# Scores one phase further ahead, PSUM copies on VectorE and a new product order in a fused attention and feed-forward kernel on Trainium2

## The chip, the cores and the metric

The kernel runs on one core of a Trainium2 chip. The core has five engines with queues of their own: TensorE (matrix products, "PE" in the profile, its weight loads "PEld"), VectorE ("DVE"), ScalarE ("ACT"), GpSimd ("POOL") and SyncE ("SP"). Each works through its instructions in program order and waits on semaphores for the others. Products land in PSUM, everything else lives in SBUF, and DMA engines move data to and from DRAM. The metric is the device time in microseconds (us) from the first to the last instruction of a run, with what lies around it. Lower is better.

## The reference

```python
def _attn_ref(q, k, v):            # 8 batches, 8 heads, 576 positions, 64 wide
    ...
    scores = scale * np.matmul(q_c, k_c.transpose(0, 1, 2, 4, 3))
    ...
    attn = np.exp(scores)
    attn = attn / (np.sum(attn, axis=-1, keepdims=True) + 1e-09)
    out = np.matmul(attn, v_c)

def _moe_ref(x, w_in, w_out, beta):
    h = x @ w_in                                # 4608x512 by 512x2048
    g = h * (1.0 / (1.0 + np.exp(-beta * h)))
    return (g @ w_out).astype(np.float32)       # by 2048x512
```

Attention runs inside chunks of 64 positions. Its 8 x 576 rows, 512 wide, go through a feed-forward layer with the activation `g`.

## The kernel before

The 4608 rows are cut into nine blocks of 512 tokens, `j` = 0 to 8; a block holds eight chunks. Every block goes through the same stages.

**Attention.** `emit_T` (L126) turns a quarter of one batch's queries and keys on VectorE. `emit_sc` (L142) makes the scores of half a block on TensorE (64 small products) into two PSUM tiles `sc0`, `sc1`, and ScalarE takes their exponentials into `et`. `emit_pv` (L174) multiplies a quarter of a block (128 tokens) by the values on TensorE, in the one PSUM tile `x`; VectorE then takes a reciprocal (L201) and scales (L203), which frees the tile; a DMA from SyncE transposes the result into `xt` (L211), the block's input to the first layer. The loads come from GpSimd's queue: `load_v` (L93), four DMAs a batch, and `load_qk` (L83), two.

**First layer, `L1` (L533).** Of the 16 hidden units (128 features each) eight are made directly: `emit_m` makes four products of 512 columns (`emit_h`, L244) and an activation on ScalarE (L254). The other eight are made by two calls of `unit` (L282), each a seven-product scheme for 2x2 blocks: bank A takes four products one upon the other, and after each of the first three a copy of the running sum is taken (`u1`, `u2`, `u3`, helper `snap`); B and C (in the tile `x`) take one and two products. The scheme needs four differences of the input, `xs` (`emit_xs`, L271, on VectorE), combines `t = u3 + w1` on GpSimd (L329) and `c1` on VectorE (L331, L335), and ends in six activations (L311). `u1` is copied by ScalarE (L306), the other copies by VectorE (L308). Direct units (`spacers`) stand between the products. A unit's bank A lies in `sc0` or `sc1`.

**Second layer, `steps_L2` (L381).** It is the seven-product scheme once more, on `g`'s halves: `mm0` to `mm6`, each of 16 products of 256 columns (L398), bank A again with running copies on ScalarE (`take`, L409), results combined on VectorE (`cB`, `cD`, `cC`, L417) and on GpSimd (`w1`, L443, and the last sum, L463). It needs sixteen sums `s1` to `s4` of `g` (`emit_sum`, four parts each): `s3` on GpSimd (L362), the others on VectorE (L358, L360, L364).

**The order** is written out by hand at L636 to L688: between the products of block `j`'s second layer stand the scores and the PV of block `j`+1. Half the scores come ahead of `mm0`, the other half after `mm1`, the four PVs after `mm1`, `mm2`, `mm3` and `mm4`; the turns of the batch after next (`tr`) stand between them, and the loads at the end. Block 0 runs a plain form of both layers, ahead of which the weights are loaded.

Of the kernel before, what the change touches and what calls it, by code (L numbers as in the profile page):

```python
# [11 lines left out]
ALU = mybir.AluOpType  # L12
# [3 lines left out]
def kernel(  # L16
# [265 lines left out]
    def unit(j, q, spacers):  # L282
        x = xt_t[j]
        ts = xs_t[j]
        up_, dn_ = slice(0, HT), slice(HT, BLK)
        b11, b21, b22 = x[:, 0:2, up_], x[:, 2:4, up_], x[:, 2:4, dn_]
        swr = [t.rearrange("p k (m i r) -> p k m r i", r=2, i=128) for t in sw]
        a11, a12, a22 = w_r[0][:, 0::2], w_r[0][:, 1::2], w_r[1][:, 1::2]
        bank = {"A": ps_s.tile([128, 2, HT], FP32, tag=f"sc{q}", name="wA")}
        xx = ps_x.tile([128, 2, 2, HT], FP32, tag="x", name="wX")  # L290
        bank["B"], bank["C"] = xx[:, 0], xx[:, 1]
        sb = {}

        def prod(b, a, rhs, first):
            for i in range(2):
                for kk in range(2):
                    nc.tensor.matmul(  # L297
                        out=bank[b][:, i, :], lhsT=a[:, kk, q, i, :], rhs=rhs[:, kk, :],
                        start=(first and i == 0 and kk == 0), stop=(kk == 1),
                        skip_group_check=True,  # L300
                    )

        def snap(nm, b, eng):
            sb[nm] = u_p.tile([128, 2, HT], FP32, tag=nm, name=nm)
            if eng == "a":
                nc.scalar.copy(out=sb[nm], in_=bank[b])  # L306
            else:
                nc.vector.tensor_copy(out=sb[nm], in_=bank[b])  # L308

        def silu(m, cols, src):  # L310
            nc.scalar.activation(  # L311
                out=gt_t[j][:, m, cols], in_=src, func=ACTF.Silu,
                scale=beta2[:, m % 2, m // 2:m // 2 + 1],
            )
# [7 lines left out]
        snap("u2", "A", "v")  # L322
        prod("C", swr[0], ts[0], True)
        snap("w1", "C", "v")
        spacers[1]()
        prod("A", swr[2], ts[2], False)
        snap("u3", "A", "v")
        sb["t"] = u_p.tile([128, 2, HT], FP32, tag="t", name="t")
        nc.gpsimd.tensor_tensor(out=sb["t"], in0=sb["u3"], in1=sb["w1"], op=ALU.add)  # L329
        prod("B", a12, b21, True)  # L330
        nc.vector.tensor_tensor(out=c1[:, :, up_], in0=bank["B"], in1=sb["u1"], op=ALU.add)  # L331
# [18 lines left out]
    def emit_sum(j, which, part):  # L350
# [2 lines left out]
        s1, s2, s3, s4 = s_t[j]  # L353
        g = gt_t[j]
        lo, hi = slice(2 * part, 2 * part + 2), slice(NM + 2 * part, NM + 2 * part + 2)
        tt = (nc.gpsimd if which == 3 else nc.vector).tensor_tensor
        if which == 1:
            tt(out=s1[:, lo], in0=g[:, lo, dn], in1=g[:, hi, dn], op=ALU.add)  # L358
        elif which == 2:
# [14 lines left out]
    def store(j, half, cols, t):  # L374
# [3 lines left out]
            in_=t,  # L378
        )

    def steps_L2(j, last=False):  # L381
        g = gt_t[j]
        t1, t2, t3, t4 = tw
# [9 lines left out]
        def prod(name, a, b, first, rows=(0, 1)):  # L393
            if first and name not in bank:
                grab(name)
            for i in rows:
                for kk in range(NM):
                    nc.tensor.matmul(  # L398
                        out=bank[name][:, i, :],
                        lhsT=a[:, kk, i * 128:(i + 1) * 128],  # L400
                        rhs=b[:, kk, :],
                        start=(first and i == 0 and kk == 0),
                        stop=(kk == NM - 1),
                        skip_group_check=True,
                    )

# [21 lines left out]
            prod("B", g[:, NM:KFF, up], b21, True)  # L428

        def mm2():  # L430
            prod("A", s_(2), t2, False)
            take("u2", "A")

        def mm3():
            prod("D", g[:, NM:KFF, dn], t4, True)

        def mm4():
            prod("A", s_(3), t3, False)
            take("u3", "A")
            if last:  # L440
                return
            sb["w1"] = u_p.tile([128, 2, HM], FP32, tag="w1", name="w1")
            nc.gpsimd.tensor_tensor(out=sb["w1"], in0=sb["u2"], in1=sb["u3"], op=ALU.subtract)  # L443

        def mm5():
            if not last:
                prod("C", s_(4), b22, True)
                return
            prod("E", s_(1), t1, True)
            for r, other in ((1, "u3"), (0, "u2")):  # L450
                if r:
                    store(j, 1, 1, comb("E", sb[other]))
                else:
# [79 lines left out]
    def L1(j, hooks={}, first=None):  # L533
# [7 lines left out]

        if first:
            first()
        emit_xs(j)
        unit(j, 0, [sp(8), sp(9), sp(10)])
        sp(11)()
        for p in (0, 2):
            emit_sum(j, 3, p)
        unit(j, 1, [sp(12), sp(13), sp(14)])
        for p in (1, 3):  # L550
# [4 lines left out]
        dve(4)  # L555
        hooks.get(KFF, lambda: None)()

    with tc.manual_schedule():
# [77 lines left out]
        for j in range(1, NB):  # L636
            na = j + 1
            hooks = {}
            if na < NB:
                hooks[KFF] = lambda: emit_sc(2 * na)  # L640
            if j == 1:
                T2 = T_items(2)
                hooks.update({9: T2[0], 11: T2[1], 13: T2[2], 15: T2[3]})
            L1(j, hooks, (lambda: emit_xp(7)) if j == 1 else None)
            at = []
            if na < NB:
                at = [
                    lambda: emit_pv(4 * na), lambda: emit_sc(2 * na + 1),
                    lambda: emit_pv(4 * na + 1), lambda: emit_pv(4 * na + 2),
                    lambda: emit_pv(4 * na + 3),  # L650
                ]
            tr = T_items(j + 2) if j + 2 < B else []
# [6 lines left out]
            mm[0]()  # L659
            while fill:  # L660
                dve()
            mm[1]()
            cB()
            go(at)
            go(at)
            emit_sum(j, 4, 0)
            emit_sum(j, 4, 1)
            mm[2]()
            go(tr)
            go(at)  # L670
            emit_sum(j, 4, 2)
            emit_sum(j, 4, 3)
            mm[3]()
            go(at)
            go(tr)
            mm[4]()
            cD()
            go(at)
            go(tr)
            mm[5]()  # L680
            if j < NB - 1:
                cC()
            go(tr)
            mm[6]()
            if j + 2 < B:
                load_v(j + 2)
            if j + 3 < B:
                load_qk(j + 3)  # L688


# [28 lines left out]
```

## Time and profile before

| what | before |
|---|---|
| median of 8 runs | 331.97 us (331.49 to 335.39) |
| the profiled execution | 331.78 us |
| its span in the trace | 330.0 us |
| around the span | 1.78 us |
| busy: TensorE, VectorE, ScalarE, GpSimd | 275.7, 222.7, 171.0, 140.0 us |
| mean granted TensorE clock | 0.984 |

The rows below are read like this. A timeline row has the start and the duration in us, the engine, the line, the operation, what it writes and reads, how many instructions are merged in it, and in brackets how long the engine sat idle before it and on whom it waited. A matmul's modelled end overlaps the next one's start, so the distance between two starts is what a product takes. A row of a table by windows has, for each stretch of the span, its length, the busy time and number of instructions of each engine, the granted clock, the DMA share and GB/s.

### The profile page before, as it was taken

How to read it: one execution, taken by the hardware profiler on the slowest of the kernel's cores; microseconds unless marked ns; L12 is line 12 of the kernel's file. 1: busy time of each engine (PE TensorE's matmuls, PEld its weight loads, DVE VectorE, ACT ScalarE, POOL GpSimd, SP SyncE). 2: the span in 40 equal slices, each digit the busy share in tenths (PEclk: the TensorE clock that was granted, in tenths of full speed). 3: DMA queues.
4: the chain of work that ended last, by engine and by line, in shares of the span. 5: the costliest groups of instructions: out<-in, count | busy, mean ns of one | idle time of the engine just before them, and what ended most of it. 6: DMA issues, size and time to landing. Idle time of an engine off the chain costs nothing.

```text
span 330.0 us, 8211 instructions
## 1 busy us (share of the span) xinstructions
PE 275.7 (84%) x3520; PEld 189.9 (58%) x3520; DVE 222.7 (67%) x377; ACT 171.0 (52%) x288; POOL 140.0 (42%) x130
## 2 busy tenths in 40 slices
PE   2889976688986998699878988899879987998695
PEld 0464433345864686468645865477547754875475
DVE  3653668859992799379836994499748565856573
ACT  1278046067347744664276526471667166716630
POOL 8622499344066415641464246431743124322430
PEclk9999999699999999999999999799999999999999
DMA  7999999400359234922493249314901310151012
GB/s 121 181 208 212 184 203 221 105 1 2 66 134 168 45 66 126 175 45 64 122 166 61 50 113 171 75 42 93 135 0 48 85 64 0 44 90 64 1 34 95
DMA packets 69589, 31.99 MB, mean 97 GB/s; under 512 B 53681, under 2 KB 63921, under 8 KB 69553
## 3 DMA queue, kind: packets, MB, share of 16 engines
q0 software_dynamic: 44960, 18.35, 45.3%
q1 hardware_dynamic: 24448, 12.99, 15.0%
q8 instruction: 27, 0.44, 0.6%
q10 hardware_dynamic: 144, 0.13, 0.1%
q14 instruction: 10, 0.07, 0.1%
HBM read 36.71 MB, written 9.44 MB: 140 GB/s over the span
## 4 chain that ended last, share of the span: by engine, by line
PE 39%; ACT 15%; POOL 14%; DMA 14%; DVE 10%; issue 6%; POOLq 0%; DVEq 0%
PE oA L398 14%; ACT gt L311 11%; DMA w_out<-in_moe_w_out_dram 10%; POOL t L329 6%; PE oD L398 4%; PE oB L398 4%; PE hps L244 4%; POOL vb L98 4%; PE wA L297 4%; DVE u L308 2%; DMA ku<-in_k_dram 2%; DMA xt<-x 2%; PE x L186 2%; PE wX L297 2%; DVE xs L277 2%
## 5 line engine op out<-in xcount | busy, mean ns | idle before, releaser
L244 PE MATMUL hps<-xt,wi 128*128 128x512 f16 (+1 forms) x336 | 82.6, 376 | 5.0 <-DMA xt<-x 3.9
L254 ACT ACTIVATE gt<-hps,beta 128x512 f16<-128x512 f32 x80 | 54.3, 688 | 44.2 <-PE hps L244 44.1
L362 POOL TENSOR_TENSOR s<-gt 128x512 f16<-128x512 f16 x32 | 39.5, 1255 | 48.0 <-ACT gt L311 48.0
L244 PEld LDWEIGHTS <-wi 128*128 128x128 f16 x336 | 32.7, 100 | 31.0 <-DMA xt<-x 5.8
L308 DVE COPY u<-wA 128x512 f32<-128x512 f32 x32 | 22.1, 691 | 41.8 <-PE wA L297 41.1
L398 PEld LDWEIGHTS <-s 128*128 128x128 f16 x496 | 46.8, 98 | 6.0
L297 PEld LDWEIGHTS <-sw 128*128 128x128 f16 x256 | 25.3, 101 | 42.6 <-issue 20.8
L398 PE MATMUL oA<-tw,s 128*128 128x256 f16 x368 | 44.1, 273 | 0.0
L297 PE MATMUL wA<-xs,sw 128*128 128x256 f16 x128 | 20.6, 286 | 28.1 <-ACT u L306 17.3
L398 PEld LDWEIGHTS <-gt 128*128 128x128 f16 x384 | 35.8, 98 | 9.2 <-ACT gt L311 4.6
L329 POOL TENSOR_TENSOR t<-u,w 128x512 f32<-128x512 f32 x16 | 20.6, 1287 | 32.1 <-DVE u L308 32.1
L443 POOL TENSOR_TENSOR w<-u,u 128x512 f32<-128x512 f32 x7 | 8.9, 1270 | 58.5 <-ACT u L409 58.5
L409 ACT COPY u<-oA 128x512 f32<-128x512 f32 x24 | 14.1, 588 | 37.5 <-PE oA L398 37.5
L98 POOL DMA_DIRECT2D vb<-in_v_dram x32 | 27.5, 876 | 8.9 <-DMA wi<-in_moe_w_in_dram 4.8
L167 ACT ACTIVATE et<-sc 128x512 f16<-128x512 f32 x34 | 18.4, 594 | 17.7 <-PE sc L158 17.6
L203 DVE TENSOR_TENSOR x<-x,rd 128x512 f16<-128x512 f32 x34 | 23.5, 691 | 1.3
L130 DVE STREAM_TRANSPOSE qT<-qu 128x576 f32<-128x576 f32 x16 | 20.0, 1250 | 5.9 <-DMA qu<-in_q_dram 5.9
L158 PE MATMUL sc<-qT,kT 32*64 32x64 f16 x1088 | 14.2, 195 | 11.6 <-DVE kT L130 6.3
L358 DVE TENSOR_TENSOR s<-gt 128x512 f16<-128x512 f16 x32 | 21.0, 656 | 4.0 <-ACT gt L311 4.0
L297 PEld LDWEIGHTS <-wi 128*128 128x128 f16 x192 | 19.0, 99 | 7.7 <-issue 0.4
L158 PEld LDWEIGHTS <-kT 32*64 32x64 f16 x1152 | 11.9, 110 | 18.0 <-issue 9.1
L130 DVE STREAM_TRANSPOSE kT<-ku 128x576 f32<-128x576 f32 x16 | 19.9, 1242 | 2.1 <-DMA ku<-in_k_dram 1.9
(81 smaller groups left out, 436.7 us busy)
## 6 DMA issues: line engine op xcount, KB each, us to landing
out_dram<-osb SPq DMA_DIRECT2D x21, 256.0 KB, 2.8
vb<-in_v_dram POOLq DMA_DIRECT2D x32, 144.0 KB, 5.1
qu<-in_q_dram POOLq DMA_DIRECT2D x7, 576.0 KB, 8.4
ku<-in_k_dram POOLq DMA_DIRECT2D x7, 576.0 KB, 10.5
out_dram<-o SPq DMA_DIRECT2D x14, 256.0 KB, 2.2
wi<-in_moe_w_in_dram POOLq DMA_DIRECT2D x4, 512.0 KB, 12.6
w_out<-in_moe_w_out_dram POOLq DMA_DIRECT2D x4, 512.0 KB, 16.9
qu<-in_q_dram POOLq DMA_DIRECT2D x2, 288.0 KB, 5.3
```

The source lines that it names most:

```text
L98: nc.gpsimd.dma_start(out=t[64 * hp:64 * hp + 64, 2 * z:2 * z + 2, :, 0:D].rearrange("p s c d -> p (s c) d"), in_=v[b, h0:h0 + 2].rearrang ...
L130: nc.vector.transpose(out=dst[b][:, z].rearrange("p t r e -> p (t r e)").bitcast(FP32).rearrange("p (t r) -> p r t", r=RUN), in_=src[b][:, ...
L158: nc.tensor.matmul(out=sc[a % 2][o0:o0 + 64, z, c, :], lhsT=kk[:, cb * CH:(cb + 1) * CH, e], rhs=qq[:, cb * CH:(cb + 1) * CH, e], start=(e ...
L203: nc.vector.tensor_tensor(out=yy, in0=src, in1=rr.to_broadcast(shape), op=ALU.mult,)
L244: nc.tensor.matmul(out=hps_t[j, m][:, c0:c1], lhsT=w_r[m // 4][:, 2 * z + e, m // 2 % 2, m % 2, :], rhs=xt_t[j][:, n, c0:c1], start=(n == ...
L254: nc.scalar.activation(out=gt_t[j][:, m, :], in_=hps, func=ACTF.Silu, scale=beta2[:, m % 2, m // 2:m // 2 + 1],)
L297: nc.tensor.matmul(out=bank[b][:, i, :], lhsT=a[:, kk, q, i, :], rhs=rhs[:, kk, :], start=(first and i == 0 and kk == 0), stop=(kk == 1), ...
L308: nc.vector.tensor_copy(out=sb[nm], in_=bank[b])
L311: nc.scalar.activation(out=gt_t[j][:, m, cols], in_=src, func=ACTF.Silu, scale=beta2[:, m % 2, m // 2:m // 2 + 1],)
L329: nc.gpsimd.tensor_tensor(out=sb["t"], in0=sb["u3"], in1=sb["w1"], op=ALU.add)
L362: tt(out=s3[:, lo], in0=g[:, lo, up], in1=g[:, lo, dn], op=ALU.subtract)
L398: nc.tensor.matmul(out=bank[name][:, i, :], lhsT=a[:, kk, i * 128:(i + 1) * 128], rhs=b[:, kk, :], start=(first and i == 0 and kk == 0), s ...
```

## The change

The scheme's `snap` always copies on VectorE, and the product B with its sum `c1` moves to second place in `unit`; the activations of bank A come ahead of those of `t`:

```diff
-        def snap(nm, b, eng):
+        def snap(nm, b):
             sb[nm] = u_p.tile([128, 2, HT], FP32, tag=nm, name=nm)
-            if eng == "a":
-                nc.scalar.copy(out=sb[nm], in_=bank[b])
-            else:
-                nc.vector.tensor_copy(out=sb[nm], in_=bank[b])
+            nc.vector.tensor_copy(out=sb[nm], in_=bank[b])
...
         prod("A", a11, b11, True)
-        snap("u1", "A", "a")
+        snap("u1", "A")
+        prod("B", a12, b21, True)
+        nc.vector.tensor_tensor(out=c1[:, :, up_], in0=bank["B"], in1=sb["u1"], op=ALU.add)
         spacers[0]()
...
         for i in range(2):
+            silu(m2 + i, up_, bank["A"][:, i])
+        for i in range(2):
             silu(m2 + i, dn_, sb["t"][:, i])
-        for i in range(2):
-            silu(m2 + i, up_, bank["A"][:, i])
```

Parts 1 and 3 of `s3` go to VectorE, the products of the second layer take `g`'s units in another order, and in bank A the third sum's product comes second:

```diff
-        tt = (nc.gpsimd if which == 3 else nc.vector).tensor_tensor
+        tt = (nc.gpsimd if which == 3 and part in (0, 2) else nc.vector).tensor_tensor
...
+    KO = (0, 1, 4, 5, 2, 3, 6, 7)
...
-                for kk in range(NM):
+                for n, kk in enumerate(KO):
...
         def mm2():
-            prod("A", s_(2), t2, False)
+            prod("A", s_(3), t3, False)
             take("u2", "A")
...
-            nc.gpsimd.tensor_tensor(out=sb["w1"], in0=sb["u2"], in1=sb["u3"], op=ALU.subtract)
+            nc.gpsimd.tensor_tensor(out=sb["w1"], in0=sb["u1"], in1=sb["u2"], op=ALU.subtract)
...
         def mm4():
-            prod("A", s_(3), t3, False)
+            prod("A", s_(2), t2, False)
             take("u3", "A")
             if last:
-                return
+                sb["w1"] = u_p.tile([128, 2, HM], FP32, tag="w1", name="w1")
+                nc.vector.tensor_tensor(out=sb["w1"], in0=sb["u1"], in1=sb["u2"], op=ALU.subtract)
+                nc.vector.tensor_tensor(out=sb["w1"], in0=sb["w1"], in1=sb["u3"], op=ALU.add)
```

In `L1` the differences `xs` are no longer made at its start, both parts of `s3` that stay on GpSimd stand after the second unit, and no sums end it. The order by hand becomes (for `j` > 1; block 1 also makes the scores that have to be ahead from then on, four halves instead of two):

```diff
+            elif tr:
+                hooks = {10: tr.pop(0), 11: tr.pop(0), 14: tr.pop(0), 15: tr.pop(0)}
+            L1(j, hooks)
...
+            if j + 3 < B and j + 3 > 3:
+                load_qk(j + 3)
             mm[0]()
+            emit_sum(j, 3, 1)
+            emit_sum(j, 3, 3)
+            if j > 1:
+                pv(0)
+            dve(4)
+            mm[1]()
+            cB()
...
+                pv(1)
             while fill:
                 dve()
+            mm[2]()
...
+                pv(2)
...
+            mm[3]()
...
+                pv(3)
+            if j > 1:
+                sc(0)
             emit_sum(j, 4, 0)
             emit_sum(j, 4, 1)
...
+            mm[4]()
             emit_sum(j, 4, 2)
             emit_sum(j, 4, 3)
+            cD()
...
             mm[5]()
             if j < NB - 1:
                 cC()
+            if j > 1:
+                sc(1)
+            if na < NB:
+                emit_xs(na)
             mm[6]()
```

Here `pv(n)` is a PV of block `j`+1 and `sc(n)` half the scores of block `j`+2; `fill` holds the eight sums `s1` and `s2`, `dve(4)` emits four of them.

The first place is ScalarE in block 2's first layer, before the change, from the first unit's last activations (`c_1520`) to those of the second unit (`c_1599`):

```order
L311 ACTIVATE gt<-c_1520,beta_112 128x512 x2
L254 ACTIVATE gt<-hps,beta_112 128x512
L306 COPY u_1604<-wA 128x512
L254 ACTIVATE gt<-hps,beta_112 128x512 x3
L311 ACTIVATE gt<-t,beta_112 128x256 x2
L311 ACTIVATE gt<-wA,beta_112 128x256 x2
L311 ACTIVATE gt<-c_1599,beta_112 128x512 x2
```

The same stretch of ScalarE now:

```order
L308 ACTIVATE gt<-c_1660,beta_112 128x512 x2
L254 ACTIVATE gt<-hps,beta_112 128x512 x4
L308 ACTIVATE gt<-wA,beta_112 128x256 x2
L308 ACTIVATE gt<-t,beta_112 128x256 x2
L308 ACTIVATE gt<-c_1737,beta_112 128x512 x2
```

The copy of the second unit's `u1` has left the queue in which it stood behind the first unit's activations.

The second place is VectorE in block 2's second layer, before, from the product B's sum (`osb<-oB`) to the first difference of the next block (`xs`):

```order
L417 TENSOR_TENSOR osb<-oB,u_1764 128x512
L201 RECIPROCAL rd<-x 128x8
L203 TENSOR_TENSOR x_1807<-x,rd 128x512
L364 TENSOR_TENSOR s_1594<-gt,s_1592 128x512 x2
L130 STREAM_TRANSPOSE qT<-qu 128x18x32
L201 RECIPROCAL rd<-x 128x8
L203 TENSOR_TENSOR x_1922<-x,rd 128x512
L364 TENSOR_TENSOR s_1594<-gt,s_1592 128x512 x2
L201 RECIPROCAL rd<-x 128x8
L203 TENSOR_TENSOR x_1963<-x,rd 128x512
L130 STREAM_TRANSPOSE kT<-ku 128x18x32
```

VectorE now, from the same sum on (`s_1803` and `s_1804` are `s1` and `s2`, `s_1806` is `s4`):

```order
L416 TENSOR_TENSOR osb<-oB,u_1838 128x512
L201 RECIPROCAL rd<-x 128x8
L203 TENSOR_TENSOR x_1906<-x,rd 128x512
L355 TENSOR_TENSOR s_1803<-gt 128x512
L357 TENSOR_TENSOR s_1804<-s_1803,gt 128x512
L355 TENSOR_TENSOR s_1803<-gt 128x512
L357 TENSOR_TENSOR s_1804<-s_1803,gt 128x512
L201 RECIPROCAL rd<-x 128x8
L203 TENSOR_TENSOR x_1952<-x,rd 128x512
L201 RECIPROCAL rd<-x 128x8
L203 TENSOR_TENSOR x_1991<-x,rd 128x512
L361 TENSOR_TENSOR s_1806<-gt,s_1804 128x512 x4
```

The turns have left this stretch, four sums have come in between the second and the third PV, and all four parts of `s4` stand behind the last PV.

The third place is GpSimd from the end of block 2 on, before (`o` is the last sum, `t` that of a unit, `s` is `s3`):

```order
L443 TENSOR_TENSOR w_1987<-u_1900,u_1985 128x512
L463 TENSOR_TENSOR o_2054<-t,o_2051 128x512
L98 DMA vb_131<-in_v_dram 64x18x64 x4
L88 DMA qu<-in_q_dram 128x2x1152
L88 DMA ku<-in_k_dram 128x2x1152
L329 TENSOR_TENSOR t<-u_2111,w_2099 128x512
L362 TENSOR_TENSOR s_2149<-gt 128x512 x2
L329 TENSOR_TENSOR t<-u_2190,w_2178 128x512
L362 TENSOR_TENSOR s_2149<-gt 128x512 x2
```

GpSimd now, over the same stretch and to the next block's `w1`:

```order
L435 TENSOR_TENSOR w_1932<-u_1838,u_1930 128x512
L466 TENSOR_TENSOR o_2206<-t,o_2203 128x512
L98 DMA vb_131<-in_v_dram 64x18x64 x4
L328 TENSOR_TENSOR t<-u_2256,w_2244 128x512
L328 TENSOR_TENSOR t<-u_2333,w_2321 128x512
L359 TENSOR_TENSOR s_2361<-gt 128x512 x2
L88 DMA qu<-in_q_dram 128x2x1152
L88 DMA ku<-in_k_dram 128x2x1152
L435 TENSOR_TENSOR w_2488<-u_2394,u_2486 128x512
```

The loads of queries and keys have moved from ahead of the first unit's `t` to behind `s3`, and `w1` now reads `u1` and `u2`, which are there two products earlier than `u3`.

More of the change, by code (lines that the diff above doesn't have):

```diff
@@ L401, in prod @@
                         rhs=b[:, kk, :],
-                        start=(first and i == 0 and kk == 0),
-                        stop=(kk == NM - 1),
+                        start=(first and i == 0 and n == 0),
+                        stop=(n == NM - 1),
                         skip_group_check=True,
@@ L449, in mm5 @@
             prod("E", s_(1), t1, True)
-            for r, other in ((1, "u3"), (0, "u2")):
+            for r, other in ((1, "u3"), (0, "w1")):
                 if r:
```

71 lines of the change are left out of this document (34 added, 37 removed).

## The prediction

> **What bounds the kernel now.** I read the busy times first, then the blocks one by one, then one block's TensorE rows for its gaps.
>
> ```profile
> PE 275.7 (84%) x3520; PEld 189.9 (58%) x3520; DVE 222.7 (67%) x377; ACT 171.0 (52%) x288; POOL 140.0 (42%) x130
> ```
>
> TensorE is busiest and VectorE next; neither is full. The table by windows, cut where a block's first product (unit 0, bank A) starts, shows how even the blocks are:
>
> ```profile
> 94.18:127.79 33.61, 28.94 (x394) 21.04 (x392) 24.70 (x42) 18.82 (x32) 14.86 (x14) 1.00 0.67 101
> ...
> 195.00:230.16 35.16, 30.50 (x395) 21.60 (x392) 24.80 (x42) 18.82 (x32) 14.85 (x14) 0.95 0.63 99
> ...
> 262.96:295.75 32.79, 28.94 (x394) 21.02 (x392) 20.71 (x37) 18.82 (x32) 10.03 (x8) 1.00 0.21 49
> 295.75:330.00 34.25, 26.27 (x202) 19.22 (x199) 18.67 (x32) 15.47 (x27) 8.77 (x7) 1.00 0.15 49
> ```
>
> Blocks 2 to 4 take 33.6 each, block 5 35.16, blocks 6 and 7 32.8, block 8 34.25 to the end. TensorE is busy for 28.94 of a block, so about 4.7 of 33.6 is waiting. Where, the TensorE rows of block 4 show:
>
> ```profile
> 161.40 0.60 PE L297 MATMUL wA<-xt,wi 128*128 128x256 f16 x4
> 163.33 1.04 PE L244 MATMUL hps<-xt,wi 128*128 128x512 f16 x4 [1.33 <-DMA xt<-x]
> 164.34 0.61 PE L297 MATMUL wA<-xs,sw 128*128 128x256 f16 x4
> ...
> 165.23 1.03 PE L244 MATMUL hps<-xt,wi 128*128 128x512 f16 x4
> 166.09 0.60 PE L297 MATMUL wA<-xs,sw 128*128 128x256 f16 x4
> ...
> 173.62 0.60 PE L297 MATMUL wA<-xs,sw 128*128 128x256 f16 x4 [2.58 <-ACT u L306]
> ...
> 177.96 1.03 PE L244 MATMUL hps<-xt,wi 128*128 128x512 f16 x4
> ...
> 179.81 0.70 PE L158 MATMUL sc<-qT,kT 32*64 32x64 f16 x63 [0.68 <-ACT gt L311]
> 180.44 2.19 PE L398 MATMUL oA<-w_out,gt 128*128 128x256 f16 x16
> 182.46 1.91 PE L398 MATMUL oB<-w_out,gt 128*128 128x256 f16 x16
> 184.30 0.32 PE L186 MATMUL x<-vb,et 64*64 64x65 f16 x16
> 184.55 0.71 PE L158 MATMUL sc<-qT,kT 32*64 32x64 f16 x64
> ```
>
> From starts: a unit's product takes 0.44 (two of them from 164.34 to 165.23), a direct unit 0.86, a second-layer product 1.84 with a PV behind it (sixteen at 0.11, about 1.75, ahead of another product), a PV 0.25, half the scores 0.64. Three waits stand out: for the transposed input at the block's start (1.33), for ScalarE's `u1` in the second unit (2.58), and at the second layer's start for the last activations (0.68, and a stall inside `oA`, which takes 2.02).
>
> **What the change does to a block.** I lay out block 4 by these durations, with t = 0 at its first product. VectorE's and ScalarE's, from the same block:
>
> ```profile
> 165.06 0.69 DVE L308 COPY u<-wA 128x512 f32<-128x512 f32 x1
> 165.67 0.68 DVE L308 COPY w<-wX 128x512 f32<-128x512 f32 x1
> ...
> 178.77 0.42 DVE L358 TENSOR_TENSOR s<-gt 128x512 f16<-128x512 f16 x1
> 179.56 0.42 DVE L358 TENSOR_TENSOR s<-gt 128x512 f16<-128x512 f16 x1
> 181.47 1.26 DVE L360 TENSOR_TENSOR s<-s,gt 128x512 f16<-128x512 f16 x1
> 182.65 1.37 DVE L358 TENSOR_TENSOR s<-gt 128x512 f16<-128x512 f16 x1
> ...
> 185.07 0.20 DVE L201 RECIPROCAL rd<-x 128x8 f32<-128x8 f32 x1
> 185.31 0.69 DVE L203 TENSOR_TENSOR x<-x,rd 128x512 f16<-128x512 f32 x1
> 185.91 0.75 DVE L364 TENSOR_TENSOR s<-gt,s 128x512 f16<-128x512 f16 x2
> 186.58 1.25 DVE L130 STREAM_TRANSPOSE qT<-qu 128x576 f32<-128x576 f32 x1
> ```
>
> ```profile
> 178.13 0.91 ACT L311 ACTIVATE gt<-t,beta 128x256 f16<-128x256 f32 x2 [0.15 <-POOL t L329]
> 178.94 0.82 ACT L311 ACTIVATE gt<-wA,beta 128x256 f16<-128x256 f32 x2
> 179.66 1.32 ACT L311 ACTIVATE gt<-c,beta 128x512 f16<-128x512 f32 x2
> 180.88 0.67 ACT L254 ACTIVATE gt<-hps,beta 128x512 f16<-128x512 f32 x1
> 181.57 1.28 ACT L167 ACT_TABLE_LOAD   x1
> ```
>
> Instructions that follow at once overlap, so starts count again: a copy or combination costs VectorE 0.61, a pair `s1`, `s2` 0.79, a pair of `s4` 0.67, a PV's two steps 0.84, a turn 1.25 less such an overlap, about 1.15. ScalarE's pairs cost 0.81, 0.72 and 1.22. A copy's result is there after 0.69, and VectorE starts 0.72 after a unit's product starts (164.34 to 165.06).
>
> *First layer.* The input and `xs` are made inside the previous second layer, so the first wait goes. Bank A's second product starts at 1.74 (A, B, one direct unit) instead of 2.94. In front of each unit's fourth product stands one new wait: `u3` must be copied before the bank is written again, and the unit's B no longer lies between. The third product starts at 3.48, the copy runs from 4.18 to 4.87, the fourth starts at 4.94 where TensorE was ready at 4.78: 0.16. The second unit's `u1` needs a copy on VectorE; a turn is queued ahead of it to 7.73, so it ends at 8.42, and TensorE waits 0.07 instead of 2.58. TensorE's last direct unit ends at 13.43, against 17.4 before (177.96 + 0.86 - 161.40): **4.0 gained**. VectorE's added copies hide in its idle first layer; without that cover they would cost 0.61 each.
>
> *The joint.* `mm0` may take 4 of its 16 products at once, the fifth needs the second unit's last activations. These follow its fourth product at 11.69: +0.72, then 0.72, 0.81 and 1.22 on ScalarE, about 15.2; eleven products of 0.11 are left, so `mm0` ends at 16.5. That is 3.1 behind the direct unit, against 3.64 before (178.82 to 182.46), of which 0.64 was scores that now stand later. **0.5 gained.** What is late here is ScalarE.
>
> *Second layer.* Here VectorE becomes the pace. Each PV waits until the one before has been scaled out of the tile `x`, and four sums now stand ahead of the third. From the last activations: two `s3` parts to 16.0; first PV to 17.8; four sums to 19.4; `cB` to 20.0; second PV to 20.85; four sums to 22.45. Beside these GpSimd now runs `w1`:
>
> ```profile
> 181.06 2.69 POOL L362 TENSOR_TENSOR s<-gt 128x512 f16<-128x512 f16 x2 [2.96 <-ACT gt L311]
> 192.08 1.27 POOL L443 TENSOR_TENSOR w<-u,u 128x512 f32<-128x512 f32 x1 [8.34 <-ACT u L409]
> ```
>
> While GpSimd made its two sums at 181.06, VectorE's 0.42 sums took 1.26 and 1.37: each ended 0.4 behind one of GpSimd's. `w1` waits for `u2`, so it runs from about 21.5 to 22.8, inside the second four sums. One of them is held: +1.1, so they end at 23.55. Its former place met only PSUM combinations. *SBUF — State Buffer* in the Trainium skill ("Who interferes with whom") says that a VectorE instruction with two SBUF inputs shares a read port with GpSimd, and the later one waits for the whole of the earlier one; the two rows agree, and without this rule the block would be 30.4.
>
> Then the third PV is scaled at 24.4; TensorE, which finished `mm3` at 23.0, may make the fourth only now (to 24.8); it is scaled at 25.8, the four `s4` end at 27.25, and `mm5` needs them. `mm5` with its switch takes to 29.1, scores to 29.75, `mm6` to **31.5**. The rest of the layer takes 15.0 where it took 12.54 (182.46 to 195.00): 2.5 given back, 0.64 of it the moved scores.
>
> The new table load and exponentials (1.28 + 1.1) between `u2` and `u3` hold `cD` to 29.2, just ahead of `cC`, which waits for `mm5` anyway; uncovered, they would cost up to 0.7. The fourth transpose is issued near 26 and, by the row below, lands near 28.6; `xs` is not due before 30.0. GpSimd's value loads still stand ahead of the next `t` and hold it by 0.5, which ScalarE's backlog hides.
>
> **The sum.** Block 2 to 4: 3 x 2.1 = 6.3. Block 5: 35.16 to 31.5, 3.7, since it carries the one slow-clock stretch (0.95), which started right behind its wait for `u1`:
>
> ```profile
> 207.22 1.01 PE L297 MATMUL wA<-xs,sw 128*128 128x256 f16 x4 [2.60 <-ACT u L306]
> ```
>
> This row is 1.01 long where the same product takes 0.60 elsewhere. The wait goes, so I let the 1.56 go too. *TensorE: Matmul & The Clock Gate* in the Trainium skill (Part 1) says the clock halves after an idle window of about 3.4 us; this gap was 2.60, and equal gaps in other blocks left the clock alone, so by the rule the cause would lie elsewhere, and keeping those 1.56 the sum would be 319.0. Block 6: 32.80 to 31.4, 1.4. Block 7 has no scores and no turns: 30.8, so 2.0. Block 8's wait for `u1` is shorter:
>
> ```profile
> 307.16 0.60 PE L297 MATMUL wA<-xs,sw 128*128 128x256 f16 x4 [1.80 <-ACT u L306]
> ```
>
> So its first layer and joint gain 3.75, not 4.5; and its tail loses 0.9, as two more combinations (0.61 each) stand on VectorE ahead of the last two `s4` and of the four output combinations: the last product must wait 0.5 for `s4`, and the combinations end 0.4 behind it. That leaves 2.85. Block 1 loses:
>
> ```profile
> 56.83 4.15 DVE L278 TENSOR_TENSOR xs<-xt,xs 128x512 f16<-128x512 f16 x1
> ```
>
> Its `xs` waits for GpSimd's weight sums until 61.6 as before, but `u1` now stands behind it on VectorE (+1.3); its second layer makes two more halves of scores, has all four turns and the sums on one VectorE, and its last exponentials hold block 2's bank (they share `sc0`). I lay block 2's first product at 96.0 instead of 94.18: -1.8; the bounds are -4 and +1.5 (the unit's own wait, gone there too).
>
> Together 6.3 + 3.7 + 1.4 + 2.0 + 2.85 - 1.8 = 14.4. The span falls from 330.0 to 315.6; with the 1.78 around it **317.4**. The profiled 331.78 stands 0.2 under the median of 331.97, so nothing is added.
>
> **The rivals.** *`w1` misses the sums, or they hide it.* Its start hangs on `u2`, within 0.7 of the sums' end. Then 1.1 less in seven blocks: 309.7. For it: VectorE may get in first. Against: both are paced by the same `mm2`.
>
> *VectorE pays full durations.* If waits break the overlap, the some 20 instructions of the second-layer chain cost 0.08 more each, 1.6 a block, and seven blocks 11.2: 328.6. For it: the chain now has more handovers with TensorE. Against: before, 185.07 to 186.58 ran overlapped among such handovers.
>
> *The transposes run into the loads, and it gets slower.*
>
> ```profile
> DMA to landing us min/median/max: 2.4/2.4/3.4
> ...
> qu<-in_q_dram POOLq DMA_DIRECT2D x7, 576.0 KB, 8.4
> ku<-in_k_dram POOLq DMA_DIRECT2D x7, 576.0 KB, 10.5
> ```
>
> The first is the input's transposes, which until now had the DMA engines without such loads. In blocks 1 to 4 the loads of queries and keys now start near 15.5, and the four transposes come at 18 to 26. A last landing up to 31.1 is free, since `xs` (1.4 for four) may end at 32.2 before `u1` suffers; each us beyond costs one. At 34.7, 8.5 after the issue, the four blocks lose 3.6 each, which eats the 14.4; beyond that it is slower, and at the 10.5 of `ku` they lose 22: 339.8. For it: 8.4 to 10.5 from 15.5 reaches 24 to 27.5. Against: by then the load is over, and blocks 5 to 8 have none.
>
> **The numbers.** Forecast (312 to 323): 0.55. No collision (under 312): 0.17. Full durations (323 to 330): 0.16. Loads in the way: 0.12, some of it still faster. Range **308.5 to 329.5**, which leaves out most of the last case. A change of 0.5% (330.3 to 333.6) is about what a measurement can tell from none: faster 0.86, same 0.06, slower 0.08.
>
> **What would show it.** TensorE without a wait for `u` over 0.3 in a block's first layer; an `oA` of `mm0` held by the activations to about 16.5; PVs that wait for VectorE's scaling; one VectorE sum of 1.2 or more beside `w1`; `mm5` held by `s4`; windows of 31.5. Wrong would be: first products that wait for `xt` or `xs` (the loads), windows of 30.4 (no collision), or VectorE rows without a gap through the whole block.

## The result, and the profile after

The changed kernel takes **320.93 us** (median of 11 runs, 319.88 to 322.14), against 332.23 for the kernel before beside it (32 runs): a ratio of 0.966, 95% interval 0.963 to 0.968. The forecast was 317.4, with 308.5 to 329.5 as its range. The profiled execution took 321.88 with a span of 320.1, 9.9 less than before; the forecast was 14.4 less. Runs more than 1.5% above the fastest of their kernel are left out of medians and ratios, which below happens only in b1, to three of its eight.

The busy times on the page of the changed kernel:

```profile
PE 276.1 (86%) x3520; PEld 191.5 (60%) x3520; DVE 227.7 (71%) x411; ACT 159.2 (50%) x270; POOL 119.5 (37%) x114
```

TensorE does the same work in a shorter span; ScalarE and GpSimd have lost some, VectorE has gained some. In the chain of waits VectorE's share went from 10% to 29%, those of ScalarE and GpSimd from 15% and 14% to 9% and 1%. The table by windows, again cut where a block's first product starts (blocks 1, 2, 4, 5, 6, 7 and 8):

```profile
53.95:102.04 48.09, 35.04 (x523) 24.52 (x521) 36.54 (x54) 20.13 (x35) 15.28 (x10) 0.86 0.46 89
102.04:133.59 31.55, 29.03 (x392) 21.17 (x392) 25.40 (x45) 17.38 (x30) 11.60 (x12) 1.00 0.75 108
...
165.13:196.65 31.52, 29.00 (x395) 21.10 (x393) 25.37 (x45) 17.64 (x30) 12.33 (x12) 1.00 0.74 108
196.65:228.14 31.49, 28.98 (x394) 21.07 (x392) 25.40 (x45) 17.64 (x30) 10.94 (x10) 1.00 0.49 71
228.14:259.28 31.14, 28.84 (x395) 21.18 (x392) 21.01 (x41) 17.63 (x30) 10.90 (x10) 1.00 0.54 71
259.28:289.06 29.78, 27.47 (x266) 19.89 (x264) 20.34 (x40) 14.18 (x25) 7.53 (x6) 1.00 0.23 54
289.06:320.10 31.04, 25.92 (x202) 19.40 (x199) 18.42 (x37) 13.00 (x24) 6.04 (x5) 0.97 0.15 51
```

Blocks 2 to 5 take 31.5, as forecast, at a full clock, block 5 too. The miss stands in the first row: block 1 takes 48.09, where it took 40.63 before. The TensorE rows of block 4:

```profile
173.49 0.60 PE L297 MATMUL wA<-xs,sw 128*128 128x256 f16 x4
...
178.69 0.60 PE L397 MATMUL oA<-w_out,gt 128*128 128x256 f16 x4
179.97 0.28 PE L397 MATMUL oA<-w_out,gt 128*128 128x256 f16 x1 [0.67 <-ACT gt L308]
180.58 1.37 PE L397 MATMUL oA<-w_out,gt 128*128 128x256 f16 x11 [0.33 <-ACT gt L308]
...
189.65 0.32 PE L186 MATMUL x<-vb,et 64*64 64x65 f16 x16 [1.20 <-DVE x L203]
...
190.65 1.92 PE L397 MATMUL oA<-tw,s 128*128 128x256 f16 x16
192.41 1.91 PE L397 MATMUL oC<-w_out,s 128*128 128x256 f16 x16
```

The first row is the second unit's second product, which waited 2.58 for ScalarE's `u1` before and now waits for nothing. `mm0` stands split as 4, 1 and 11 products by ScalarE's last activations. The fourth PV waits 1.20 for VectorE's scaling of the third. `mm5` (`oC`) follows `mm4` without a gap. VectorE's rows for the same stretch:

```profile
186.93 0.42 DVE L355 TENSOR_TENSOR s<-gt 128x512 f16<-128x512 f16 x1
187.38 1.37 DVE L357 TENSOR_TENSOR s<-s,gt 128x512 f16<-128x512 f16 x1
...
190.76 0.69 DVE L203 TENSOR_TENSOR x<-x,rd 128x512 f16<-128x512 f32 x1 [0.53 <-DMA xt<-x]
191.37 1.42 DVE L361 TENSOR_TENSOR s<-gt,s 128x512 f16<-128x512 f16 x4
```

And GpSimd's row beside them:

```profile
186.98 1.49 POOL L435 TENSOR_TENSOR w<-u,u 128x512 f32<-128x512 f32 x1 [5.01 <-ACT u L408]
```

The last of the eight sums takes 1.37 instead of 0.42 and ends just behind `w1`: the collision that the sum counted with 1.1, measured 0.95. The row of 190.76 shows something the forecast had only as a rival, and at another place: the fourth PV's scaled result waits for a transposition, since the tile `x` of L203 has three buffers and the first PV's is still being read.

TensorE at the end of block 1's second layer shows the miss:

```profile
89.64 0.45 PE L158 MATMUL sc<-qT,kT 32*64 32x64 f16 x32 [0.47 <-DVE kT L130]
93.90 0.32 PE L158 MATMUL sc<-qT,kT 32*64 32x64 f16 x8 [3.81 <-DVE kT L130]
94.15 3.59 PE L397 MATMUL oC<-w_out,s 128*128 128x256 f16 x16
97.54 3.10 PE L397 MATMUL oA<-tw,s 128*128 128x256 f16 x16
100.57 0.71 PE L158 MATMUL sc<-qT,kT 32*64 32x64 f16 x64
102.04 0.60 PE L297 MATMUL wA<-xt,wi 128*128 128x256 f16 x4 [0.77 <-ACT et L167]
```

And VectorE's last turn there:

```profile
92.61 1.24 DVE L130 STREAM_TRANSPOSE kT<-ku 128x576 f32<-128x576 f32 x1
```

The change puts half of block 3's scores ahead of `mm5`, and the last eight of them need the fourth turn of batch 3, which VectorE ends at 93.85. TensorE stands still for 3.81; then `oC` and `oA` take 3.39 and 3.03 from start to start where they take 1.84 and 1.76 elsewhere. The clock was halved there: from 94.15 to 100.57 the granted clock is 0.55. (The 0.86 of the whole block has a second such stretch in it, behind the wait for `xs` that was there before.)

### The profile page after: what moved, and what is told of

Read it like the earlier page. It is cut to its first block, busy times and chain, and to the rows that moved or that the text cites. A ratio compares the mean times of both kernels' runs of the same rounds, so it can differ in the third digit from the quotient of the medians.

```text
span 320.1 us, 8248 instructions
## 1 busy us (share of the span) xinstructions
PE 276.1 (86%) x3520; PEld 191.5 (60%) x3520; DVE 227.7 (71%) x411; ACT 159.2 (50%) x270; POOL 119.5 (37%) x114
## 4 chain that ended last, share of the span: by engine, by line
PE 43%; DVE 29%; DMA 12%; ACT 9%; issue 5%; POOL 1%; DVEq 0%; ACTq 0%; POOLq 0%
PE oA L397 12%; PE hps L244 11%; DMA w_out<-in_moe_w_out_dram 10%; ACT gt L308 7%; PE wA L297 6%; DVE x L203 5%; DVE s L357 5%; PE wX L297 4%; PE oC L397 4%; DVE s L355 3%; DVE kT L130 3%; PE sc L158 3%; DVE qT L130 2%; DMA ku<-in_k_dram 2%; DVE osb L416 2%
## 5 line engine op out<-in xcount | busy, mean ns | idle before, releaser
L244 PE MATMUL hps<-xt,wi 128*128 128x512 f16 (+1 forms) x336 | 81.1, 371 | 0.8 <-ACT xt L223 0.7
L254 ACT ACTIVATE gt<-hps,beta 128x512 f16<-128x512 f32 x80 | 52.6, 684 | 25.7 <-PE hps L244 25.4
L397 PEld LDWEIGHTS <-s 128*128 128x128 f16 x496 | 48.1, 100 | 8.0 <-DVE s L361 0.3
L305 DVE COPY u<-wA 128x512 f32<-128x512 f32 x48 | 33.0, 688 | 17.6 <-PE wA L297 17.5
L397 PE MATMUL oA<-tw,s 128*128 128x256 f16 x368 | 45.3, 278 | 0.0
L466 POOL TENSOR_TENSOR o<-t,o 128x512 f32<-128x512 f32 x7 | 8.9, 1267 | 68.1 <-ACT o L463 68.1
L297 PE MATMUL wA<-xs,sw 128*128 128x256 f16 x128 | 19.6, 276 | 6.9 <-DVE u L305 6.9
L203 DVE TENSOR_TENSOR x<-x,rd 128x512 f16<-128x512 f32 x34 | 23.5, 691 | 2.7 <-DMA xt<-x 1.6
L435 POOL TENSOR_TENSOR w<-u,u 128x512 f32<-128x512 f32 x7 | 10.2, 1457 | 39.6 <-ACT u L408 34.2
L397 PE MATMUL oA<-w_out,gt 128*128 128x256 f16 x128 | 17.7, 274 | 7.0 <-ACT gt L308 7.0
L158 PEld LDWEIGHTS <-kT 32*64 32x64 f16 x1152 | 12.1, 111 | 16.4 <-DVE kT L130 12.5
```

The costliest lines, as they stand in the source:

```text
L158: nc.tensor.matmul(out=sc[a % 2][o0:o0 + 64, z, c, :], lhsT=kk[:, cb * CH:(cb + 1) * CH, e], rhs=qq[:, cb * CH:(cb + 1) * CH, e], start=(e ...
L203: nc.vector.tensor_tensor(out=yy, in0=src, in1=rr.to_broadcast(shape), op=ALU.mult,)
L244: nc.tensor.matmul(out=hps_t[j, m][:, c0:c1], lhsT=w_r[m // 4][:, 2 * z + e, m // 2 % 2, m % 2, :], rhs=xt_t[j][:, n, c0:c1], start=(n == ...
L254: nc.scalar.activation(out=gt_t[j][:, m, :], in_=hps, func=ACTF.Silu, scale=beta2[:, m % 2, m // 2:m // 2 + 1],)
L297: nc.tensor.matmul(out=bank[b][:, i, :], lhsT=a[:, kk, q, i, :], rhs=rhs[:, kk, :], start=(first and i == 0 and kk == 0), stop=(kk == 1), ...
L397: nc.tensor.matmul(out=bank[name][:, i, :], lhsT=a[:, kk, i * 128:(i + 1) * 128], rhs=b[:, kk, :], start=(first and i == 0 and n == 0), st ...
```

## The experiments

Eleven kernels ran. The first is the kernel before with one edit, the others are the changed kernel, or another run that is named, with one edit; e5 joins three.

| run | median us (runs) | ratio to before | 95% interval |
|---|---|---|---|
| b1_u1_on_vector | 328.73 (5) | 0.989 | 0.985 to 0.993 |
| e1_block1_scores_last | 317.79 (4) | 0.957 | 0.955 to 0.959 |
| e2_w1_on_vector | 318.45 (4) | 0.959 | 0.958 to 0.961 |
| e3_u1_on_scalar | 333.06 (10) | 1.002 | 0.999 to 1.004 |
| e4_w1_vector_four_x | 315.57 (4) | 0.948 | 0.944 to 0.953 |
| e5_best | 312.50 (4) | 0.939 | 0.934 to 0.944 |
| e6_all_s3_on_gpsimd | 324.24 (4) | 0.974 | 0.971 to 0.978 |
| e8_loads_in_first_layer | 315.88 (4) | 0.949 | 0.945 to 0.953 |
| e9_units_in_order | 321.92 (4) | 0.967 | 0.962 to 0.973 |
| e10_B_fourth | 322.16 (4) | 0.969 | 0.964 to 0.973 |
| e11_best_fewer_sums_early | 309.30 (4) | 0.930 | 0.927 to 0.934 |

### Where the gain hangs: the copy of `u1`

**The copy undone** (e3):

```diff
-            nc.vector.tensor_copy(out=sb[nm], in_=bank[b])
+            if nm == "u1":
+                nc.scalar.copy(out=sb[nm], in_=bank[b])
+            else:
+                nc.vector.tensor_copy(out=sb[nm], in_=bank[b])
```

> The changed kernel, but u1 is copied by ScalarE again, all else as changed. Theory (ScalarE's queue is the place of the old wait): the second unit's second product waits again, about 1.8 us (its u1 copy stands behind the first unit's activations and the direct unit's), and since the last activations follow, a block rises from 31.5 to about 33.3: 12 to 15 us more than the changed kernel, that is about the time of the kernel before. Rival (with B second and xs early there is room enough): under 0.5 a block, under 4 us in all.

In the total the whole gain is gone, as expected: 12.1 us more than the changed kernel. TensorE's row in the second unit of block 4 of this run, and blocks 1 and 4 by windows:

```profile
176.42 0.60 PE L297 MATMUL wA<-xs,sw 128*128 128x256 f16 x4 [1.57 <-ACT u L306]
```

```profile
53.09:100.62 47.53, 34.59 (x523) 24.12 (x521) 35.26 (x52) 21.10 (x37) 15.26 (x10) 0.89 0.51 92
...
166.35:199.61 33.26, 29.24 (x394) 21.00 (x392) 24.27 (x43) 18.83 (x32) 12.38 (x12) 1.00 0.71 102
```

The wait is back, and block 4 takes 33.26 (about 33.3 was expected). But the total hides something. Block 1 loses 6.9 here as well (47.53 against 40.63 before). Blocks 2 to 8 together take 229.0, where they took 235.8 before the change and take 218.1 in the changed kernel. So without the copy the rest of the change is worth 6.8 in these blocks, some 1.6 of it block 5's stretch of half clock, which did not come; block 1 eats it up. The copy on top of it is worth 10.9 there.

**The copy alone** (b1, on the kernel before):

```diff
-        snap("u1", "A", "a")
+        snap("u1", "A", "v")
```

> The kernel before with one edit: a unit's u1 is copied by VectorE instead of ScalarE. Theory (the wait for u1 is a wait in ScalarE's queue, behind the first unit's activations): in the second unit TensorE's second product starts 0.07 to 0.2 after it could, not 2.58, and what is late next is GpSimd, whose two s3 parts stand ahead of the second t: the last activations come about 1.9 earlier in each of eight blocks, so 15 us less, about 317 us. Rival (the wait only moves: the joint at the second layer's start or the wait for the transposed input takes it over): the second unit runs earlier, but a block stays within 0.5 of 33.6, so 328 to 332 us.

It gains 3.2 us by the medians (331.90 before, beside it), 1.1% by the ratio, against 11.3 and 3.4% for the change. The expected 317 is missed, and the total is the rival's. But the wait moved mainly to a place that the rival did not name: the second unit no longer waits, and in the first unit the copy now stands behind `xs` on VectorE. Two blocks of this run by windows, and rows of TensorE and VectorE in the second of them:

```profile
92.07:124.29 32.22, 28.84 (x394) 21.08 (x392) 25.99 (x44) 17.84 (x30) 14.84 (x14) 1.00 0.69 105
124.29:158.19 33.90, 30.52 (x394) 21.75 (x392) 26.09 (x44) 17.72 (x30) 14.82 (x14) 0.95 0.66 100
```

```profile
125.31 1.04 PE L244 MATMUL hps<-xt,wi 128*128 128x512 f16 x4 [0.42 <-DMA xt<-x]
128.53 0.60 PE L297 MATMUL wA<-xs,sw 128*128 128x256 f16 x4 [2.19 <-DVE u L308]
...
129.41 1.77 PE L244 MATMUL hps<-xt,wi 128*128 128x512 f16 x4
130.97 1.06 PE L297 MATMUL wA<-xs,sw 128*128 128x256 f16 x4
```

```profile
127.46 0.42 DVE L280 TENSOR_TENSOR xs<-xt,xs 128x512 f16<-128x512 f16 x1
127.80 0.69 DVE L308 COPY u<-wA 128x512 f32<-128x512 f32 x1
```

Of blocks 2 to 7, three have an even clock and take 32.2 to 32.9 (33.6 before); in the other three the clock halves behind the wait for `u`, and they take 33.9. So the two parts need each other: in blocks 2 to 8 the rest of the change alone (e3) is worth 6.8, the copy alone (b1) 3.2, and both together 17.8. The copy takes the second unit's wait away. In the changed kernel `xs` is made in the previous second layer, so that the copy on VectorE has nothing in front of it. VectorE in block 4, which starts at 165.13, waits for the product itself:

```profile
165.77 0.69 DVE L305 COPY u<-wA 128x512 f32<-128x512 f32 x1 [0.71 <-PE wA L297]
```

No run separates what the earlier scores, the earlier PVs and the earlier place of `xs` each bring.

### The miss: block 1's scores

```diff
-            if j == 1:
-                sc(0)
             mm[5]()
...
             if j == 1:
+                sc(0)
                 sc(1)
```

> The changed kernel, but block 1 makes both halves of block 3's scores behind mm6 instead of one half ahead of mm5. Theory (block 1 loses its 6 us because these scores stand on TensorE ahead of mm5 and wait for the last turn on VectorE, and the pause then halves the clock): no wait of 3.8 ahead of mm5, no products at half clock in mm5 and mm6 of block 1; block 2's first product 4 to 5 us earlier than at 102.0, the run 4 to 5 us faster than the changed kernel. Rival (VectorE has too much work in block 1, whatever the order): mm5 still starts near 94 and the run gains under 1.5 us.

TensorE in this run, at the same place:

```profile
91.05 1.91 PE L397 MATMUL oA<-tw,s 128*128 128x256 f16 x16
92.89 0.88 PE L158 MATMUL sc<-qT,kT 32*64 32x64 f16 x64
...
96.47 1.01 PE L297 MATMUL wA<-xt,wi 128*128 128x256 f16 x4 [0.76 <-ACT et L167]
```

The scores find their turns done, `mm5` starts at 88.40 instead of 94.15 (so the rival falls), `mm5` and `mm6` run at full clock, and block 2 starts at 96.47 (forecast for the change: 96.0). Block 1 falls from 48.09 to 42.97. Block 2 gives 1.5 back (33.09), in a stretch of half clock behind three waits for the exponentials, of which the last row shows one. The span is 4.0 shorter, the median 3.1, where 4 to 5 were expected.

### The collision of `w1` with the sums, and what it covered

**`w1` on VectorE**, just ahead of `cD` (e2):

```diff
-            sb["w1"] = u_p.tile([128, 2, HM], FP32, tag="w1", name="w1")
-            nc.gpsimd.tensor_tensor(out=sb["w1"], in0=sb["u1"], in1=sb["u2"], op=ALU.subtract)
...
         def cD():
+            if not last:
+                sb["w1"] = u_p.tile([128, 2, HM], FP32, tag="w1", name="w1")
+                nc.vector.tensor_tensor(out=sb["w1"], in0=sb["u1"], in1=sb["u2"], op=ALU.subtract)
```

> The changed kernel, but the second layer's w1 is made by VectorE just ahead of cD (where it waits for u3 anyway) instead of by GpSimd beside the sums. Theory (collision): the sum that took 1.37 takes 0.42, the fourth PV's wait for VectorE falls from 1.20 to about 0.25, a block of 2 to 6 falls from 31.5 to 30.6, block 7 likewise: 5 to 6 us less than the changed kernel. Rival (TensorE or ScalarE set the pace of the second layer anyway): blocks fall by under 0.3, under 2 us in all.

The fourth PV waits 0.26 instead of 1.20 (PVs wait for L203 by 2.2 in all, 7.9 in the changed kernel), but only blocks 5 to 7 profit, and the run gains 2.5 us where 5 to 6 were expected. Blocks 2 and 5 by windows:

```profile
100.78:132.69 31.91, 29.27 (x393) 20.94 (x392) 24.99 (x46) 17.38 (x30) 10.13 (x11) 1.00 0.75 107
...
195.87:226.46 30.59, 29.02 (x394) 21.20 (x392) 25.04 (x46) 17.64 (x30) 9.44 (x9) 1.00 0.51 73
```

In block 2, a row of VectorE, one of TensorE, and the issue of the first PV's transposition by SyncE:

```profile
126.91 0.69 DVE L203 TENSOR_TENSOR x<-x,rd 128x512 f16<-128x512 f32 x1 [1.97 <-DMA xt<-x]
```

```profile
127.99 0.39 PE L397 MATMUL oC<-w_out,s 128*128 128x256 f16 x2 [0.80 <-DVE s L361]
```

```profile
118.90 1.20 SPq L211 DMA_TRANSPOSE xt<-x  x1
```

The wait for the transposition has grown to 1.97: VectorE gets the buffer at 126.91, 8.0 after that issue. It holds `s4` behind it, and `mm5` waits for `s4`. Without the collision this second wait comes first in blocks 2 to 4, those whose second layer loads queries and keys.

**Two ways to take that wait away**, each on top of e2: a fourth buffer (e4), or the loads of batches 5 to 7, until now in the second layer of blocks 2 to 4, in the first layer there (e8).

```diff
-    x_p = ctx.enter_context(tc.tile_pool(name="x", bufs=3))
+    x_p = ctx.enter_context(tc.tile_pool(name="x", bufs=4))
```

```diff
+                if j + 3 < B:
+                    hooks[11] = lambda f=hooks[11], b=j + 3: [f(), load_qk(b)]
...
-            if j + 3 < B and j + 3 > 3:
-                load_qk(j + 3)
+            if j == 1:
+                load_qk(4)
```

> The changed kernel with w1 on VectorE (the run e2_w1_on_vector, 318.45 us) and four buffers of the tile x instead of three. Theory: in blocks 2 to 4 the fourth PV's scaling waits only because its buffer is still read by the first PV's late transpose; with a fourth buffer that wait (up to 1.97 in e2) goes, blocks 2 to 4 fall from 31.5-31.9 to about 30.6, in all about 3 us: 315.5. Rival: the late transposes come out at another place (xs, or the next block's first product waits for xt), or TensorE sets the pace there: no gain, 318 to 319.

> e2_w1_on_vector (318.45 us) with the loads of the next queries and keys issued in the first layer for blocks 5 to 7 (block 4's stay where they are), three buffers of x as before. Theory: the first PV's transpose lands late because it is issued 1 to 3 us behind these loads; without them the fourth PV's wait for xt<-x (0.6 to 1.97) is gone in the blocks whose loads moved, which fall to about 30.6: 316 to 316.7. Rival: the wait stays, since it comes from the buffers alone: 318 to 319.

Both bring what was expected (315.57 for 315.5; 315.88 for 316 to 316.7, a hair better). Block 3 of e4, then block 3 of e8, by windows:

```profile
131.23:161.69 30.46, 28.89 (x394) 21.07 (x392) 25.14 (x48) 17.64 (x30) 10.83 (x11) 1.00 0.81 112
```

```profile
133.26:163.83 30.57, 29.00 (x395) 21.11 (x393) 25.01 (x46) 17.64 (x30) 10.80 (x11) 1.00 0.75 112
```

Blocks 2 to 5 take 30.5 to 30.6 in both runs, and neither has a wait of L203 for `xt` left. In e8 the buffers are as before, so it is the loads that make the first PV's transposition late; in e4 the loads are as before, so the lateness costs nothing but through the buffer.

**The collision from the other side**: all of `s3` on GpSimd (e6).

```diff
-        tt = (nc.gpsimd if which == 3 and part in (0, 2) else nc.vector).tensor_tensor
+        tt = (nc.gpsimd if which == 3 else nc.vector).tensor_tensor
```

> The changed kernel with all four parts of s3 on GpSimd instead of two. Theory (VectorE's two-input sums are held while GpSimd makes one): parts 1 and 3 of s3 now run on GpSimd beside the first four s1 and s2, each 0.42 sum beside them takes 1.2 to 1.4, so every block loses 0.8 to 1.2 less the 0.7 that VectorE is spared: 323 to 330. Rival (the sums run side by side): VectorE's second layer is 0.7 shorter in each block, 315 to 321.

In the total the theory, in the blocks only half of it. Block 4 of this run, VectorE, then GpSimd:

```profile
184.30 1.26 DVE L357 TENSOR_TENSOR s<-s,gt 128x512 f16<-128x512 f16 x1
```

```profile
182.73 2.55 POOL L359 TENSOR_TENSOR s<-gt 128x512 f16<-128x512 f16 x2
...
242.46 4.56 POOL L359 TENSOR_TENSOR s<-gt 128x512 f16<-128x512 f16 x4
```

In blocks 2 to 4 the loads stand between GpSimd's parts, the last two run to 185.3 beside the sums, one of these is held, and the block takes 32.3 (+0.8). In blocks 5 to 7 (second GpSimd row) all four parts end at 247.0, before the first sum at 247.3: nothing is held, and the blocks take 31.5, 31.2 and 29.8, as in the changed kernel. The price follows the overlap, not the operation. VectorE's 0.7 of spared work gave nothing there, as the first PV behind `mm0` sets the start of the chain. So moving half of `s3` to VectorE, a part of the change, is worth 0.8 in each of three blocks and nothing in blocks 5 to 7.

### Two small parts of the change undone

**The order of `g`'s units** (e9) and **the place of the product B** (e10):

```diff
-    KO = (0, 1, 4, 5, 2, 3, 6, 7)
+    KO = (0, 1, 2, 3, 4, 5, 6, 7)
```

```diff
-        prod("B", a12, b21, True)
-        nc.vector.tensor_tensor(out=c1[:, :, up_], in0=bank["B"], in1=sb["u1"], op=ALU.add)
         spacers[0]()
...
+        prod("B", a12, b21, True)
+        nc.vector.tensor_tensor(out=c1[:, :, up_], in0=bank["B"], in1=sb["u1"], op=ALU.add)
         spacers[2]()
```

> The changed kernel with the second layer's products taking g's units in their natural order. Theory: the joint is paced by ScalarE's last activations, and the order of the change lets two more of mm0's products (0.11 each) stand ahead of that wait: without it the blocks take 0.22 longer, 31.5 becomes 31.75 and the whole 1.5 us more (322.4). Rival: VectorE sets the pace behind mm0, and the order is worth nothing: 31.5 and 320.9.

> The changed kernel with the product B and its sum back in their former place behind the third product; all copies stay on VectorE. Theory: the copy of u1 takes 0.72 + 0.69 from the start of the unit's product, and without B only 1.30 lies between, so the second product waits 0.1 in the first unit and some 0.5 in the second (a turn is queued ahead); the fourth product's 0.16 in each unit goes in turn. Blocks between 31.5 and 31.9, in all 320.5 to 324. Rival (B second is what makes the copies free): the second product waits for u1 by 1 us or more in both units, blocks over 33, 332 or more.

`mm0` of e9 in block 4, and the second unit's second product of e10:

```profile
180.21 0.28 PE L397 MATMUL oA<-w_out,gt 128*128 128x256 f16 x1 [0.89 <-ACT gt L308]
180.82 1.59 PE L397 MATMUL oA<-w_out,gt 128*128 128x256 f16 x13 [0.33 <-ACT gt L308]
```

```profile
173.67 0.60 PE L297 MATMUL wA<-xs,sw 128*128 128x256 f16 x4 [0.40 <-DVE u L305]
```

With the natural order 13 products stand behind the wait instead of 11, and blocks 2 to 5 take 31.71 to 31.75: 0.2 each, as expected, though the two ratios, 0.967 and 0.966, don't resolve it. B in its old place costs two waits for `u1`, 0.09 and 0.40, and saves one of 0.20 for `c` and two of 0.1; blocks 2 to 5 take 31.56 to 31.68. The move of B is worth less than 0.1 in five of blocks 2 to 7 and 0.16 in block 4: the gain is the copy's, not B's.

### The version that beats both

e5 joins e1, e2 and e4's buffer. e11 adds one edit for the other long wait of block 1: one of GpSimd's weight sums is made behind unit 0's `t`.

```diff
         emit_tw(2)
-        emit_tw(4)
         emit_tw(3)
...
-                hooks = {9: T2[0], 11: T2[1], 13: T2[2], 15: T2[3], KFF: lambda: emit_sc(4)}
+                hooks = {9: T2[0], 11: lambda: [emit_tw(4), T2[1]()], 13: T2[2], 15: T2[3], KFF: lambda: emit_sc(4)}
```

> Scores of block 1 behind mm6, w1 on VectorE, four buffers of x, all three together. If the three act apart from one another: 320.9 less 3.1 (block 1's scores) less 2.5 (w1) less 3 (buffers of x): 312.3. If the fourth buffer brings nothing: 315.3. A value over 316 would say that block 1 and the collision share what they cost.

> The run e5_best (312.5 us) with one of GpSimd's four weight sums (tw 4, first needed by mm3) made behind unit 0's t of block 1 instead of ahead of it. Theory (VectorE's sums with two SBUF inputs are held while GpSimd makes one): block 1's xs then meet two weight sums instead of three; the row of 4.15 falls to 0.4, the first second-layer-of-sums product of block 1 starts 4.1 earlier, and the stretch of half clock behind that wait goes or shrinks: 306.5 to 308.5. Rival (xs is late because of its own input, or what comes first is late as well): under 1 us, 311.5 to 312.5.

e5 took 312.50 where 312.3 was expected: the three act apart, as far as its runs tell (311.30 to 314.03; block 1 takes 44.09 in its profile, 1.1 more than in e1). e11 took 309.30, 3.2 less, and misses the 306.5 to 308.5. Its rows, GpSimd, VectorE, TensorE:

```profile
52.37 4.09 POOL L369 TENSOR_TENSOR tw<-w_out 128x2048 f16<-128x2048 f16 x1
```

```profile
54.45 2.30 DVE L277 TENSOR_TENSOR xs<-xt 128x512 f16<-128x512 f16 x1 [0.17 <-ACT xt L223]
56.78 0.43 DVE L278 TENSOR_TENSOR xs<-xt,xs 128x512 f16<-128x512 f16 x1
```

```profile
58.53 0.60 PE L297 MATMUL wA<-xs,sw 128*128 128x256 f16 x4 [3.00 <-DVE u L305]
...
59.76 1.81 PE L244 MATMUL hps<-xt,wi 128*128 128x512 f16 x4
```

The held row of 4.15 is now 0.43, and the product starts 3.7 earlier than in e5 (62.20). But the stretch of half clock stays, though the wait is 3.00 instead of 6.86: the last row has 1.81 for a unit that elsewhere shows 1.03.

## Why the prediction was right, and where it was off

**The first layer and the joint: right.** The second unit's second product waits for nothing, the waits at the fourth products are 0.1 each (0.16 in the forecast), one of 0.20 for the sum `c` was not in it, and `mm0` is held as laid out: block 4's first PV starts 16.75 after the block's first product (16.5). e3 shows that the larger part of the gain hangs on the copy, b1 that the copy needs the earlier `xs`, which the forecast took for granted when it let both waits go at once.

**The second layer: right in its pace.** The fourth PV waits for the scaling, at 24.52 of the block (forecast 24.4 to 24.55), `mm5` starts at 27.28 (27.3), the block ends at 31.5. One step was wrong, and the 27.3 a coincidence: `mm5` is not held by the four `s4`, which end at 27.66, but follows TensorE's own `mm4`. It can, since its first products need only the first of the four parts. e2 shows the wait for `s4` as soon as the scaling is later.

**The rival of no collision** fell: the 1.37 beside `w1` is there. (In its two rows from before, the forecast read VectorE's sums as ending 0.4 behind GpSimd's; it is 0.28, as here.) The estimate of a block without it, 30.4, is 30.5 to 30.6 in e4. **Full durations** fell: VectorE's rows still start 0.61 apart. **The loads in the way** was true as a mechanism and small: 0.53 in block 4, 1.6 in three blocks by the waits, and that hidden behind the collision. It works through the buffers of `x`, which the forecast did not name, not through `xs`.

**The half clock of block 5** went with its wait, as let go. The rule of the Trainium skill (*TensorE: Matmul & The Clock Gate*, Part 1) puts the drop behind an idle window of some 3.4 us. Here half clock followed on gaps of 2.60 (before), 0.42 and 2.19 close together (b1), 3.00 (e11), and 0.75, 0.30 and 0.76 close together (e1), so the measurement decides.

**Block 1 was mis-sized**, outside its own bounds. Forecast: block 2's first product at 96.0, a loss of 1.8, at worst 4. Measured: 102.04, a loss of 7.9, of which 0.4 lay ahead of block 1. The step counted "two more halves of scores" and "all four turns" as VectorE's and TensorE's work, and did not ask which turn the scores ahead of `mm5` need: the last one. e1 shows that this alone was some 5, a good half of it (2.8) the half clock behind the pause.

**The last blocks were better.** Block 7 took 29.78 (30.8): without its two halves of scores, 0.64 each, it is 1.36 shorter than block 6, where the forecast took off only 0.6. Blocks 6 and 8 were 0.3 and 0.4 better; why was not followed up. For the total these 1.7 are luck: they hide a part of block 1's miss.

So the sum: 14.4 forecast; block 1 -5.7 and its later start -0.4; blocks 2 to 5 -0.1; block 6 +0.3, block 7 +1.0, block 8 +0.4: 9.9, as the spans differ.

## What to carry to other kernels

When work is pulled a phase ahead, ask of each instruction that is now issued early which producer is last, in the first block above all, where producers still catch up: one early product behind a late turn cost some 5 us, nearly the 6.2 that three later blocks gained. A move of a PSUM copy to another queue pays in full only if what stands ahead of it there is early too; the two belong in one change. When a part is undone, compare the blocks and not only the totals: e3's total equals that of the kernel before, while its blocks do not. And after a fix, look for the second wait of nearly the same length under the first: here a buffer stood right under the collision.

## What the runs showed of the hardware

The clock is halved behind waits shorter than one would guess, and not always. Before the change the gap of 2.60 in block 5 was followed by it, equal ones in blocks 2 to 4 were not. In b1 a wait of 2.19 in block 3 was followed by it and one of 2.23 in block 2 was not, at a price of 1.67 (33.90 against 32.22). The five runs of b1 spread from 326.51 at a granted clock of 0.973 to 330.63 at 0.957, while the eleven of the changed kernel, with no wait over 1.3 after block 1, stay within 2.3.

A VectorE sum with two SBUF inputs is held until 0.28 to 0.30 behind the end of GpSimd's instruction and not longer: 2.30 from 54.45 beside a weight sum that ends at 56.46 (e11), and 0.43 right behind it; 4.15 where another weight sum follows. *SBUF — State Buffer* in the Trainium skill ("Who interferes with whom") says so, and these rows agree.
